# Block-sparse attention and an MLP on one core: the same operations in another order, with VectorE and GpSimd set differently against each other

## The chip, the cores and the metric

The kernel runs on one core of a Trainium2 chip. A core has five engines that work side by side, each through its own list of instructions in order: TensorE (PE in the profile; PEld is its loading of weights), VectorE (DVE), ScalarE (ACT), GpSimd (POOL) and SyncE (SP), which here only issues transfers. They wait for each other through semaphores. The metric is the device time of one execution in microseconds (us).

## The reference

Attention over q, k, v of shape (4, 8, 768, 64), then an MLP on its output. The keys are cut into 12 blocks of 64. For each query the mean key of every block gives a gate score; blocks later than the query's own are shut out; the three best blocks, and the query's own, are seen, causally:

```python
k_rep = k.reshape(B, H, n_blocks, block, D).mean(axis=3)
gate_scores = np.einsum('bhsd,bhnd->bhsn', q, k_rep)
gate_scores = np.where(causal, gate_scores, -1000000000.0)
top_idx = np.argsort(gate_scores, axis=-1)[..., -top_k:]
...
scores = np.where(mask, scores, -1000000000.0)   # mask: chosen or own block, and causal
attn = softmax(scores);  out = attn @ v
...
h = x @ w_in                                     # x: 3072 x 512, w_in: 512 x 2048
g = 0.5 * h * (1.0 + np.tanh(c * (h + 0.044715 * h * h * h)))
return (g @ w_out).astype(np.float32)            # w_out: 2048 x 512
```

## The kernel before

The work is tiled by pairs of heads: 4 batches of 4 pairs, pair p = 0 to 15. For each pair a preparation (`pre`) turns q and k so that the head dimension lies on the partitions, makes the block means, the gate scores, and from them the mask. After the four pairs of a batch its 768 tokens go through the MLP, while the next batch's pairs are prepared and attended.

The preparation of a pair, step by step, with the engine and the line in the file of before:

- the loads of k, q and v (`load`, L387 and L393, issued on SP). The first batch's are turned by PE (L541), with copies out of PSUM on DVE or ACT (`copy`, L356 on ACT, L358 on GpSimd, L360 on DVE). Later batches' q and k are turned by DVE (L557).
- block sums of the keys (L576, L614, DVE) and their place in a two-head matrix `ksb` (L582, L588, L631, DVE).
- the gate scores: eight small matmuls (L680, PE).
- the selection, on DVE: a transpose (L696, called gx below), adding the causal gate `cgate` (L703), the eight largest of each row (L712), a comparison with the third of them (L713), and the mask value `madd` with the own block let in by `ownm1` (L717). L703, L713 and L717 are two-input steps: both operands lie in SBUF.
- the mask, transposed by PE (L749; later batches by a transfer) and copied below the queries as 12 further rows, so that the score matmul adds it. The matching rows of the keys hold a constant matrix E, which says to which block a key belongs; SP copies it there (`fill`, L513).

The attention of a pair: score matmuls (L856 for batch 0, L1039 later), exp on ACT (L875, L1052), a causal cut of the diagonal blocks on GpSimd (`affine_select`, L901 and L1066, tile `ats`), the product with v (L924, L1078), the division by the sum (L942 and L943, L961 and L962, DVE), and a transpose of the output into the MLP's input `xT` (L981, PE).

The MLP: first product (L1115), gelu on ACT (L1127), second product. Batch 0 does this plainly (L1315). The others use seven products instead of eight for a 2 x 2 split (L1365, with sums of weights L1284 and of activations L1302 on DVE, and joins of the results L1414); batch 3 does part of its first product so too (L1163 to L1228). The weights `w_in` and `w_out` are each loaded in two halves from GpSimd's queue (`load_w`, L451 and L453). The load of `w_in` is started by a tiny copy on GpSimd that reads the last v of batch 0. On SP, a small transfer that reads the end of `w_in` (`hold`, L1560) keeps the loads of pair 4 and later back until `w_in` is there.

GpSimd also makes the constants: `emit_p(i)` zeroes the parts of buffer set i that nothing else writes (four memsets over L502 to L507), `gates` makes `cgate` and `ownm1` (L473 to L484), `e16` makes E (a memset L491 and two `affine_select` of L494).

Finally `warm` offers 72 matmuls on zeros (L1517); those that the order names keep TensorE busy in the beginning and fill some gaps.

What sets the order of everything is three tables written out in the file. Each step is an operation with a number. `ORDER` lists the numbers; `BUFFER` holds, in that order, which buffer a step takes where there are several; `ENGINE` names the steps that run on ACT or GpSimd in place of their first choice. Nothing is reordered afterwards: each engine, and each engine's queue of transfers, works in the order in which `Plan.run` emits.

```python
for n in ORDER:
    op = self.ops[n]
    for kind, key in op.takes:
        if key not in self.buf:
            self.buf[key] = self.kinds[kind][0][next(picks)]
    op.emit(engine.get(n, next(iter(op.engines))))
```

Of the kernel before, what the change touches and what calls it, by code (L numbers as in the profile page):

```python
# [182 lines left out]
    "POOL": [  # L183
        338, 586, 587, 646, 647, 707, 708, 972, 973, 1035, 1036, 1097, 1098,
        1159, 1160, 1425, 1426, 1488, 1489, 1550, 1551, 1612, 1613]}


class Op:
# [1431 lines left out]
```

## Time and profile before

| | before |
|---|---|
| median of 3 runs | 253.98 us (253.59 to 254.15) |
| the profiled execution | 254.11 us |
| its span, first to last instruction | 252.4 us |
| granted TensorE clock | 1.00 |
| busy: PE / DVE / ACT / POOL | 244.2 / 188.6 / 178.5 / 86.8 us |

The span is what the profile's rows cover; 1.7 us of the execution lie around it. A row of a timeline gives start, duration, engine, line, operation, the tiles out<-in, the shape, a count where several are drawn together, and in brackets how long the engine was idle before it and what ended that. A list of waits gives who waited for whom, total, times and the longest. A row of windows gives the busy time of each engine in a stretch. A row of a group gives the shortest, median and longest duration in ns.

### The profile page before, as it was taken

To read this page: it belongs to the slowest core of one execution; us is meant where nothing else is said; L and a number is where in the kernel's file an instruction comes from. 1 tells how busy PE (TensorE), PEld (TensorE's weight loads), DVE (VectorE), ACT (ScalarE), POOL (GpSimd) and SP (SyncE) were. 2 spreads that over 40 slices of the span, in tenths; PEclk is the share of its full clock that TensorE was granted. 3 is DMA by queue.
4 is the path that set the end of the run, shared out by engine and by line. 5 is a ranking of instruction groups with operands and counts; after the bars stand their busy time and mean duration, and the time that the engine had idled before them with its cause. 6 is when DMAs were issued, how large, how long until landed. Compare 5 with 4: busy or idle time off the path is not lost.

```text
span 252.4 us, 6423 instructions
## 1 busy us (share of the span) xinstructions
PE 244.2 (97%) x2483; PEld 170.4 (68%) x2483; DVE 188.6 (75%) x533; ACT 178.5 (71%) x225; POOL 86.8 (34%) x169
## 2 busy tenths in 40 slices
PE   7898999999999999999999999999999999999993
PEld 5665786555546666555778887656778887666883
DVE  2799863031869999999898977999775785687954
ACT  2577877546799999767899897757998927667300
POOL 8766860002135587240066644420244500000000
PEclk9999999999999999999999999999999999999999
DMA  8999599999999895999998996351601250020024
GB/s 153 219 207 184 88 211 180 214 151 160 141 153 130 155 198 93 146 176 181 167 204 145 223 154 114 88 118 42 166 4 24 41 180 20 3 84 0 4 92 158
DMA packets 130927, 32.62 MB, mean 129 GB/s; under 512 B 124528, under 2 KB 126928, under 8 KB 130896
## 3 DMA queue, kind: packets, MB, share of 16 engines
q1 hardware_dynamic: 126160, 27.62, 64.7%
q0 software_dynamic: 3136, 4.19, 10.0%
q10 hardware_dynamic: 1600, 0.39, 0.8%
q8 instruction: 19, 0.31, 0.6%
q14 instruction: 12, 0.10, 0.1%
HBM read 27.26 MB, written 6.29 MB: 133 GB/s over the span
## 4 chain that ended last, share of the span: by engine, by line
PE 91%; DVE 4%; DMA 2%; issue 1%; ACTq 1%; ACT 0%; DVEq 0%
PE wide L1115 27%; PE bank L1365 22%; PE wide L1039 11%; PE bank L1315 8%; PE bank L1078 6%; PE wide L1204 5%; PE wide L856 3%; PE bank L680 2%; PE bank L924 2%; DMA G<-in_q_dram 2%; PE bank L541 1%; PE bank L749 1%; PE bank L981 1%; DVE sel L712 1%; DVE sel L713 1%
## 5 line engine op out<-in xcount | busy, mean ns | idle before, releaser
L1115 PE MATMUL wide<-xT,w_in 128*128 128x384 f16 x416 | 74.1, 326 | 0.0
L1052 ACT ACTIVATE ats<-wide 128x896 f16<-128x896 f32 x72 | 62.0, 913 | 3.6 <-PE wide L1039 1.3
L1127 ACT ACTIVATE G<-wide 128x768 f16<-128x768 f32 x52 | 42.0, 809 | 27.0 <-PE wide L1115 25.3
L1115 PEld LDWEIGHTS <-w_in 128*128 128x128 f16 x416 | 39.9, 98 | 26.8 <-issue 1.3
L1066 POOL TENSOR_SCALAR_AFFINE_SELECT ats<-ats 128x256 f16<-128x256 f16 x72 | 31.3, 450 | 58.1 <-ACT ats L1052 57.8
L1039 PE MATMUL wide<-qT,kT 76*128 76x512 f16 (+3 forms) x192 | 38.6, 305 | 0.0
L557 DVE STREAM_TRANSPOSE s<-sd 128x768 f32<-128x768 f32 x24 | 23.2, 970 | 13.7 <-DMA sd<-in_k_dram 11.5
L1365 PE MATMUL bank<-w_out,G 128*128 128x256 f16 x216 | 31.9, 272 | 0.0
L1365 PEld LDWEIGHTS <-G 128*128 128x128 f16 x288 | 27.2, 98 | 5.2
L1315 PE MATMUL bank<-w_out,G 128*128 128x512 f16 x96 | 28.1, 379 | 0.0
L1414 DVE TENSOR_TENSOR osb<-bank,osb 128x512 f32<-128x512 f32 (+1 forms) x38 | 22.2, 594 | 7.0 <-PE bank L1365 6.5
L1039 PEld LDWEIGHTS <-kT 76*128 76x128 f16 x192 | 17.3, 97 | 10.6 <-issue 0.5
L875 ACT ACTIVATE ats<-wide 128x1024 f16<-128x1024 f32 (+3 forms) x24 | 21.0, 916 | 4.7 <-PE wide L856 4.6
L1078 PEld LDWEIGHTS <-ats 128*128 128x128 f16 x504 | 21.8, 97 | 3.6 <-POOL ats L1066 0.2
L358 POOL CAST kT<-s 64x768 f16<-64x768 f32 x23 | 19.5, 846 | 14.0 <-DVE s L557 13.2
L1078 PE MATMUL bank<-v,ats 128*128 128x65 f16 x504 | 24.1, 194 | 0.0
L1365 PEld LDWEIGHTS <-XS 128*128 128x128 f16 x216 | 20.0, 97 | 4.8
L1365 PE MATMUL bank<-TS,XS 128*128 128x256 f16 x144 | 22.8, 272 | 0.0
L358 POOL CAST v<-vsd 128x768 f16<-128x768 f32 x13 | 10.7, 828 | 30.9 <-DMA vsd<-in_v_dram 22.2
L356 ACT CAST qT<-s 64x768 f16<-64x768 f32 x21 | 17.4, 827 | 0.3
L962 DVE TENSOR_TENSOR xn<-bank,zr 128x384 f16<-128x384 f32 x24 | 13.4, 558 | 0.8
L712 DVE MAX8 sel<-sel 128x8 f32<-128x12 f32 x160 | 13.3, 157 | 0.6
(118 smaller groups left out, 350.3 us busy)
## 6 DMA issues: line engine op xcount, KB each, us to landing
out_dram<-osb SPq DMA_DIRECT2D x23, 256.0 KB
vsd<-in_v_dram SPq DMA_DIRECT2D x26, 192.0 KB
sd<-in_k_dram SPq DMA_DIRECT2D x48, 96.0 KB
sd<-in_q_dram SPq DMA_DIRECT2D x48, 96.0 KB
w_in<-in_moe_w_in_dram POOLq DMA_DIRECT2D x2, 1024.0 KB, 11.3
w_out<-in_moe_w_out_dram POOLq DMA_DIRECT2D x2, 1024.0 KB, 18.5
G<-in_q_dram SPq DMA_DIRECT2D x4, 192.0 KB
G<-in_k_dram SPq DMA_DIRECT2D x4, 192.0 KB
```

The lines of the kernel that those rows point to most:

```text
L358: nc.gpsimd.tensor_copy(out=out, in_=in_)
L557: nc.vector.transpose(out=T[key + "T32", p], in_=T[key, p].rearrange("p t j -> p (t j)"))
L875: nc.scalar.activation(out=T["at", u][:, :, 0:n], in_=plan.buf[("st",) + u].rearrange("p (h w) -> p h w", h=2)[:, :, 0:n], func=AF.Exp, bi ...
L1039: nc.tensor.matmul(st[:, x:e], kT16[i][h][0:76, s0:s0 + 128], qT16[i][h][0:76, s0 + (x - cb):s0 + (e - cb)], start=True, stop=True)
L1052: nc.scalar.activation(out=T["at", u][:, 0:n], in_=plan.buf[("st",) + u][:, 0:n], func=AF.Exp, bias=0.0, scale=SCALE)
L1066: nc.gpsimd.affine_select(out=dg, in_=dg, compare_op=ALU.is_ge, fill=0.0, base=0, pattern=[[0, 2], [1, 128]], channel_multiplier=-1)
L1078: nc.tensor.matmul(pvv[:, qc, 0:65], at[:, cb + (qc - jc) * 128: cb + (qc - jc + 1) * 128], v16[i][:, jc, h, :], start=(gi == 0 and jc == ...
L1115: nc.tensor.matmul(hps[:, 512 * e:512 * e + HALF], w_in16[:, ci, (2 * j + e) * 128: (2 * j + e + 1) * 128], T["xT", b][:, ci, HALF * h:HAL ...
L1127: nc.scalar.activation(out=G[:, :, h, j, :], in_=plan.buf["hps", b, j, h].rearrange("p (e w) -> p e w", e=2)[:, :, 0:HALF], func=AF.Gelu_a ...
L1315: nc.tensor.matmul(plan.buf["ops", b, ti], G[:, f % 2, 2 * ti // NC, f // 2, ti % (NC // 2) * 128:ti % (NC // 2) * 128 + 128], w_out16[:, ...
L1365: nc.tensor.matmul(dst[:, HD * h:HD * h + HD], FACT[m][0][:, j, t * 128:(t + 1) * 128], FACT[m][1][:, j, :], start=(clear and j == 0), sto ...
L1414: nc.vector.tensor_tensor(out=dst(), in0=src(), in1=other(), op=ALU.add)
```

## The change

Only the three tables change; the functions and so the operations are the same, and the file is one line shorter, so that line numbers after the tables are smaller by one. The core of the diff, the beginning of `ORDER` and all of `ENGINE`:

```diff
 ORDER = [
-    5, 2, 1890, 6, 1891, 1892, 1893, 9, 15, 0, 1894, 1895, 1896, 1897, 12,
-    1898, 1899, 1900, 22, 1901, 1902, 1903, 23, 1904, 1905, 1906, 71, 72,
-    62, 73, 195, 64, 63, 82, 75, 76, 66, 1907, 3, 77, 1908, 74, 1, 18, 1909,
...
+    1890, 3, 9, 1891, 1892, 1893, 1894, 1, 6, 15, 1895, 2, 1896, 1897, 1898,
+    195, 1899, 1900, 1901, 1902, 1903, 1904, 1905, 1906, 12, 1907, 71, 62,
+    64, 73, 72, 75, 0, 82, 76, 66, 77, 63, 1908, 1909, 74, 22, 23, 1910, 67,
+    1911, 98, 18, 68, 1912, 84, 85, 19, 100, 78, 31, 99, 194, 83, 79, 101,
...
     "ACT": [
-        63, 67, 74, 99, 101, 114, 119, 121, 345, 346, 349, 449, 467, 486,
-        504, 523, 541, 594, 595, 628, 654, 657, 715, 716, 719, 749, 893,
-        980, 981, 1043, 1044, 1105, 1106, 1167, 1168, 1202, 1433, 1434,
-        1496, 1497, 1558, 1559, 1668, 1674, 1677, 1704, 1707, 1727, 1733,
-        1736, 1786, 1822],
+        63, 67, 72, 74, 90, 94, 99, 101, 119, 121, 134, 331, 346, 449, 467,
+        486, 504, 523, 541, 594, 628, 654, 655, 657, 715, 716, 749, 929,
+        980, 981, 1043, 1044, 1105, 1106, 1167, 1202, 1346, 1433, 1434,
+        1496, 1668, 1677, 1698, 1704, 1727, 1733, 1736, 1786, 1822],
     "POOL": [
-        338, 586, 587, 646, 647, 707, 708, 972, 973, 1035, 1036, 1097, 1098,
-        1159, 1160, 1425, 1426, 1488, 1489, 1550, 1551, 1612, 1613]}
+        337, 586, 587, 646, 647, 707, 708, 972, 973, 1035, 1036, 1097, 1098,
+        1159, 1160, 1426, 1488, 1489, 1550, 1551, 1612, 1613]}
```

What this does to each engine's list, by the numbers:

- GpSimd's constants. Before: `emit_p(3)` (5), `emit_p(0)` (2), `gates` (0), `emit_p(1)` (3), `e16` (1), `emit_p(2)` (4), then cuts of `ats` and casts. After: `emit_p(1)` (3), `e16` (1), `emit_p(0)` (2), `gates` (0), one cut of `ats` (197), `emit_p(3)` (5), `emit_p(2)` (4), and the rest. The load of `w_out` (163) is issued behind three more cuts than before.
- SP's loads after the first five. Before: q2, k2, v0, half of k3, half of q3, half of k3, v1, half of q3, v2, v3. After: half of k2, q2, half of k2, v0, v1, q3, half of k3, half of v2, half of k3, half of v2, v3. Later loads change places as well (k6's first half ahead of q5, for instance).
- PE: the gate of pair 2 (122) stands behind one more product with v (208), one product with v (315) ahead of the first L1115; steps of the first batch change places throughout. 35 of the matmuls on zeros are used instead of 37; the two left out stood between real work.
- From ACT to DVE: 114 (a copy of k), 345, 595, 1168, 1497, 1558, 1559 (q as 16-bit, pairs 4 to 14), 349, 719 (mask copies of pairs 4 and 7), 893 (a result of the second product), 1674, 1707 (intermediate results of batch 3). From DVE to ACT: 72 (q of pair 0), 90, 94, 134 (k of pairs 1 and 3), 331 (`xT`), 655 (q as 16-bit, pair 6), 929, 1346 (results of the second product), 1698. From DVE to GpSimd: 337; from GpSimd to DVE: 338, 1425 (k as 16-bit).
- The end: the same steps in the same chain.

295 rows, old and new, of tables (BUFFER, ORDER) are left out of this document.

## The prediction

> **What bounds the kernel now.** I read the busy times first, then the windows, then the waits of TensorE, and last the timelines at the places the waits name. The page's first part, for the whole span:
>
> ```profile
> PE 244.2 (97%) x2483; PEld 170.4 (68%) x2483; DVE 188.6 (75%) x533; ACT 178.5 (71%) x225; POOL 86.8 (34%) x169
> ```
>
> PE is missing 8.2 us of 252.4. The windows (time, then width and PE busy, PEld, DVE, ACT, POOL, clock, DMA share, GB/s) show where:
>
> ```profile
> 5.00:10.00 5.00, 3.50 (x35) 2.75 (x33) 3.20 (x13) 1.44 (x3) 4.62 (x11) 1.00 1.37 219
> 15.00:20.00 5.00, 4.36 (x67) 2.96 (x65) 4.75 (x20) 4.61 (x6) 2.68 (x5) 1.00 0.97 207
> 20.00:25.00 5.00, 4.20 (x81) 3.07 (x76) 4.72 (x20) 3.28 (x4) 3.58 (x6) 1.00 1.05 180
> 75.00:150.00 75.00, 74.96 (x794) 51.42 (x793) 70.55 (x192) 66.88 (x86) 35.83 (x65) 1.00 1.05 165
> 240.00:252.40 12.40, 8.61 (x79) 7.47 (x77) 5.72 (x11) 0.00 (x0) 0.00 (x0) 1.00 0.35 127
> ```
>
> PE has holes in the front and in the tail; between them it is full, at full clock. So time can be won only in the front or by giving PE less to do; time can be lost wherever another engine falls behind. DVE is the one with little room: 70.55 of 75 us. The longest waits of PE (total, times, longest):
>
> ```profile
> PE bank L749 <- DVE madd L717: 1.8, 3, 0.8
> PE bank L1517 <- DVE bmask L285: 1.1, 1, 1.1
> PE bank L541 <- DMA G<-in_q_dram: 0.8, 1, 0.8
> ```
>
> The mask transposes (L749) wait for the selection chain on DVE (L696, L703, L712, L713, L717). In DVE's rows for that chain in the first pair, and then for three calls of L713 in 11 to 24 us (durations in ns):
>
> ```profile
> L703 DVE TENSOR_TENSOR sel<-sel,cgate x1: 714/714/714, 7.9 to 7.9; 128x48 f32<-128x48 f32 x1
> L713 DVE TENSOR_TENSOR sel<-sel,sel x1: 509/509/509, 9.1 to 9.1; 128x48 f32<-128x48 f32 x1
> L717 DVE SCALAR_TENSOR_TENSOR madd<-sel,ownm x1: 207/207/207, 9.7 to 9.7; 128x48 f16<-128x48 f32 x1
> ```
>
> ```profile
> L713 DVE TENSOR_TENSOR sel<-sel,sel x3: 234/285/750, 12.1 to 21.8; 128x120 f32<-128x120 f32 x2, 128x72 f32<-128x72 f32 x1
> ```
>
> A larger L713 (128x72) takes 0.23 us and 128x48 takes 0.51; the same 128x120 takes 0.285 or 0.75. GpSimd's rows of the same times:
>
> ```profile
> 6.88 0.74 POOL L491 MEMSET G<- 128x768 f16 x1
> 7.69 1.87 POOL L494 TENSOR_SCALAR_AFFINE_SELECT G<-G 64x768 f16<-64x768 f16 x2
> 9.62 0.16 POOL L502 MEMSET v<- 128x12 f16 x1
> 9.66 0.65 POOL L503 MEMSET madd<- 128x640 f16 x1
> ```
>
> The slow L703 starts at 7.9 and ends with the first of the two L494 (about 8.6); the slow L713 (9.11 to 9.62) ends with the second (9.56). L717 runs at 9.7 under a memset and is not held. So a DVE step with both inputs in SBUF stands still while GpSimd reads SBUF, and not while it only writes.
>
> **A rule beside this.** The Trainium skill, "SBUF — State Buffer", section "Who interferes with whom", says just this of two-input steps, and adds that whichever engine issues first keeps the port while the other blocks entirely. By that addition a held GpSimd would also hand its delay on; no row here shows a long held GpSimd instruction, and the sum below does without it.
>
> **The change, part by part.** All three tables are replaced; the instructions are the same but for two warm fillers.
>
> *GpSimd's constants.* Now: zeroing of buffers 3 and 0, gates, buffer 1, E, buffer 2. After: buffer 1, E, buffer 0, gates, then the first ats select, buffers 3 and 2. E (0.74 + 1.87) moves ahead of the first selection, whose start is given by PE. In the first chain L703 loses 714 − 234 = 0.48 and L713 509 − 234 = 0.28, 0.76 together (234 ns is a larger tile's time, so this is a floor). Gates comes last of the four and its own short selects may hold L703 a little: I take 0.7. The place of buffers 3 and 2 (memsets) behind the first ats select delays a cast of the mask by about 2.8 us at 13.4 us; its readers, the scores of pair 1, stand from 18 us on: nothing lost.
>
> *Front order and loads.* The rows that date the front now (two selections starting, a mask, the first v's landing):
>
> ```profile
> 14.06 0.35 DVE L696 STREAM_TRANSPOSE sel<-bank 128x160 f32<-128x160 f32 x1
> ...
> 20.26 0.34 DVE L696 STREAM_TRANSPOSE sel<-bank 128x160 f32<-128x160 f32 x1
> ```
>
> ```profile
> 9.99 0.29 PE L749 MATMUL bank<-ident,madd 128*128 128x128 f16 x2 [0.74 <-DVE madd L717]
> ...
> 31.25 0.45 PE L749 MATMUL bank<-ident,madd 128*128 128x128 f16 x5 [0.24 <-DVE madd L717]
> ```
>
> ```profile
> 16.83 0.83 POOL L358 CAST v<-G 128x768 f16<-128x768 f32 x1 [2.00 <-DMA G<-in_v_dram]
> ```
>
> On SP v1, q3 and v2's first half now go ahead of k3 or its second half. The loads take about 0.925 us per 192 KB half (estimate: from the first v, landed at 16.83, to the last, at 26.08 in the row below, are ten halves), so k3 lands at about 23.3, four halves later than now (19.6). Following the selections by hand with these rows' durations, mine is: first mask 9.2 to 9.3 (now 9.99), selection of pair 1 at 13.3 (now 14.06), of pair 2 at 19.0 (now 20.26; its gate stands behind one pv more), k3 23.3, gate 3 about 26.3, mask 3 about 29.0 (now 31.25), first MLP matmul (L1115) about 36.0 (now 38.24). A lead of 2.2 us, between 1 and 2.6. It's spent on weights:
>
> ```profile
> 26.08 0.19 POOL L451 COPY after_in<-vsd 1x16 f32<-1x16 f32 x1 [1.06 <-DMA vsd<-in_v_dram]
> 26.63 1.66 POOL L453 DMA_DIRECT2D w_in<-in_moe_w_in_dram  x2 [0.35 <-issue]
> ...
> 30.70 1.78 POOL L453 DMA_DIRECT2D w_out<-in_moe_w_out_dram  x2
> ```
>
> ```profile
> DMA to landing us min/median/max: 9.1/11.3/13.5
> ```
>
> ```profile
> DMA to landing us min/median/max: 16.1/18.5/21.0
> ```
>
> The first of these lines is w_in's, the second w_out's. w_in's second half is issued at 27.54 and lands at 41.0, w_out's first half at 30.70 + 16.1 = 46.8. The w_in issue waits for the last v load, which is last on SP in both orders, so it doesn't move. w_out's issue moves behind three more ats selects on POOL, to about 35; its data follow w_in's on the same queue, so it lands when it did as long as it's issued before w_in has landed at 41. PE now:
>
> ```profile
> 38.24 0.81 PE L1115 MATMUL wide<-xT,w_in 128*128 128x384 f16 x4
> ...
> 42.88 5.04 PE L1115 MATMUL wide<-xT,w_in 128*128 128x384 f16 x30
> 47.75 0.38 PE L1315 MATMUL bank<-w_out,G 128*128 128x512 f16 x1
> ```
>
> The pitch of L1115 is (47.75 − 42.88)/30 = 0.162. L1315, the first reader of w_out, comes 9.51 us after the first L1115, after the change 9.26 (one pv of 0.25 goes ahead of it). Started at 36.0, PE would want w_in's second half at 40.4, wait to 41.1, want w_out at 46.0, wait to 46.8. The work done by then is the same as at 47.75 now: of 2.2 us of lead **0.95** stays. Any lead of over 1 us gives the same.
>
> *Fillers.* 37 zero matmuls become 35; the two missing stood between real work, at about 0.11 each (the pitch of matmuls of the same 128x256, in the chain's last stretch): **−0.2**, from PE's full time.
>
> ```profile
> 232.31 16.20 PE bank L1365 x148
> ```
>
> *Copies changed over.* Twelve go from ACT to DVE (six of them q16, 0.56 each in the row below), nine the other way, one more comes to DVE from GpSimd; by the durations the same operations have in the trace DVE gets 2.5 us more. The place where this can reach PE is the last gate of batch 2:
>
> ```profile
> L360 DVE CAST qT<-s x3: 552/556/556, 77.7 to 188.6; 64x768 f16<-64x768 f32 x3
> ```
>
> ```profile
> 63.40:115.20 51.80, 51.76 (x492) 30.59 (x491) 47.19 (x143) 45.27 (x60) 24.80 (x42) 1.00 1.03 149
> ```
>
> ```profile
> 115.06 0.14 DVE L631 TENSOR_TENSOR ksb<-bmask,ks 128x32 f32<-128x32 f32 x1
> ```
>
> ```profile
> 114.95 0.79 PE L680 MATMUL bank<-s,ksb 128*32 128x160 f32 x16
> ```
>
> These are the gates of pairs 10 and 11, eight matmuls each, 0.31 apiece and overlapping: the second begins about 115.3, its ksb is ready at 115.2, so 0.1 us is left. After the change PE reaches this gate 0.5 us earlier counted from pair 4's, and DVE has 0.2 more to do (one q16 and two mask copies more, one q16 and one transpose for the weights less, one w_sums step more), while about 0.3 us of DVE's waiting for PE goes. 0.5 + 0.2 − 0.1 − 0.3 gives 0.3; with port holds as now, which grow where DVE has more two-input steps in GpSimd's company, I take **+0.5**. Bounds: 0, if DVE's 4.6 us of idle in that window give way, and 0.3 + 2.3 = 2.6, if a wait for a gate like the one now ahead of pair 5 is met once more:
>
> ```profile
> 71.48 0.35 DVE L696 STREAM_TRANSPOSE sel<-bank 128x160 f32<-128x160 f32 x1 [2.26 <-PE bank L680]
> ```
>
> *The tail* has the same chain: nothing.
>
> Sum: 254.11 − 0.95 − 0.2 + 0.5 = 253.46 for the profiled execution, which was 0.13 over the median of 253.98: **253.3**.
>
> **The rivals.** (a) The cap doesn't hold: with less on the DMA queues w_out lands a us or so earlier, or the later POOL issue matters less than I think. Then the whole lead of 2.2 counts: 252.1. Against it: nothing in the change moves w_in's issue. (b) The front wins nothing: k3's landing 3.7 us later holds gate 3 by more than I walked, and L1115 starts at 38.2 as now; 254.11 − 0.2 + 0.3 − 0.13 gives 254.1. For it: in the row of waits, loads already hold PE by 0.8. (c) The other side: DVE becomes the bound. It has 4.45 us idle in 75 to 150 us and takes on a part of the 2.5 us there. If the gate of pair 11 is missed by the upper bound, 2.6, what PE loses there isn't found again, as PE has no later hole: 254.11 − 0.95 − 0.2 + 2.6 − 0.13 = 255.4. It decides from a miss of 1.7 us (0.95 + 0.2 won, 0.5 of measurement); beyond 2.6 lies 256. (d) w_out's issue slips behind 41 us, because the ats selects ahead of it on POOL wait for exps that wait for PE: then each us of slip is a us of PE, and 5 us of slip lose all; with 36.85 as the present time of the last of these three selects it takes a front 4 us slower than now.
>
> **How the numbers follow.** The forecast, its terms within 0.5 us, gets 0.42; (a) 0.13; (b) 0.17; (c) 0.23; (d) 0.05. Range 252.2 to 255.8: it leaves out (d), the worst of (c) and a full uncapped lead. The likeliest case's own range is 252.8 to 253.9. A measurement of this kernel can tell about 0.2%, 0.5 us, from no change: faster means under 253.47, slower over 254.49. Faster: most of the forecast's case and (a), 0.46; same: the rest of it and most of (b), 0.21; slower: (c), (d) and a part of (b), 0.33.
>
> **What would show it.** Right: L703 and L713 of the first pair at about 0.23; L1115's first start near 36 and waits of PE for w_in and w_out, some 0.7 and 0.8, that the list now lacks; the first L1315 at 46.8; 35 L1517; in 75 to 150 us a new wait of PE for ksb of under a us. Wrong: first L1115 after 37.3; L1315 before 46.5; waits of PE for DVE that sum to over 1.7 us after 38 us.

## The result, and the profile after

The changed kernel is slower: 256.25 us (median of 6, 255.39 to 257.21) against 253.83 (median of 6), ratio 1.0095, 95% interval 1.0068 to 1.0123. The forecast was 253.3, range 252.2 to 255.8, and faster. The profiled execution of the changed kernel took 257.21 us, the slowest of the six, with a span of 255.5; what follows is its trace, 0.96 us over the median: shares of a loss that are read from it hold for this execution. Lines of the changed file are smaller by one.

Its busy times, and the slices of TensorE's granted clock:

```profile
PE 246.6 (97%) x2481; PEld 170.5 (67%) x2481; DVE 191.9 (75%) x537; ACT 175.0 (69%) x222; POOL 88.5 (35%) x168
...
PEclk9999999999999999999999999999979999999998
```

DVE is busy 3.3 us longer and ACT 3.5 less, near the forecast's 2.5 and a part of it holding. One slice of the clock, near 188 us, is new, and the last one is lower. The waits of PE:

```profile
PE bank L1077 <- POOL ats L1065: 1.6, 2, 1.1
PE bank L1516 <- DVE bmask L284: 1.1, 1, 1.1
PE bank L540 <- DMA G<-in_q_dram: 0.9, 1, 0.9
PE wide L1038 <- DVE qT L359: 0.4, 1, 0.4
PE bank L1364 <- DVE XS L1301: 0.3, 1, 0.3
PE bank L748 <- DVE madd L716: 0.3, 1, 0.3
PE bank L1314 <- DMA w_out<-in_moe_w_out_dram: 0.2, 1, 0.2
PE wide L1203 <- DVE s L359: 0.2, 1, 0.2
```

The mask wait (L748, 1.8 before) is down to 0.3. In its place stand waits that the list of before lacks, and the largest is for the causal selects of GpSimd (L1065). First the front, where the forecast looked. The first pair's selection, durations in ns, and PE around the start of the MLP:

```profile
L702 DVE TENSOR_TENSOR sel<-sel,cgate x1: 208/208/208, 8.0 to 8.0; 128x48 f32<-128x48 f32 x1
L712 DVE TENSOR_TENSOR sel<-sel,sel x1: 207/207/207, 8.7 to 8.7; 128x48 f32<-128x48 f32 x1
```

```profile
36.31 2.44 PE L1114 MATMUL wide<-xT,w_in 128*128 128x384 f16 x14
...
40.70 5.04 PE L1114 MATMUL wide<-xT,w_in 128*128 128x384 f16 x30
45.95 0.38 PE L1314 MATMUL bank<-w_out,G 128*128 128x512 f16 x1 [0.21 <-DMA w_out<-in_moe_w_out_dram]
```

The two steps that took 0.71 and 0.51 take 0.21 each. The first L1114 starts at 36.31 (38.24 before, and a product of 0.25 now lies ahead of it), the first reader of w_out at 45.95 (47.75): a lead of 1.8 us. PE keeps it: the first matmul of the second product of batch 1 starts at 119.75, against 121.90 before, 2.15 earlier. Then it goes. The first matmul of the second product of batch 2 starts at 176.47 against 177.31, 0.84 earlier; its first matmul of product 7 at 189.36 against 186.87, 2.5 later; the last join at 251.64 against 248.54, 3.1 later. So 1.3 us are lost between 120 and 176, 3.3 between 176 and 189, and 0.6 behind that; of this last part only one wait of 0.2 (L1203) stands on the list, and the rest was not followed up.

The 3.3 us, in rows of GpSimd, VectorE and PE:

```profile
180.74 4.07 POOL L1065 TENSOR_SCALAR_AFFINE_SELECT ats<-ats 128x256 f16<-128x256 f16 x3 [10.41 <-ACT ats L1051]
```

```profile
180.62 1.01 DVE L1301 TENSOR_TENSOR XS<-G,XS 128x768 f16<-128x768 f16 x2
181.56 1.48 DVE L1301 TENSOR_TENSOR G<-G 128x768 f16<-128x768 f16 x3
182.96 0.67 DVE L1413 TENSOR_TENSOR osb<-bank,osb 128x512 f32<-128x512 f32 x1
183.56 0.54 DVE L1301 TENSOR_TENSOR G<-G 128x768 f16<-128x768 f16 x1
184.13 0.85 DVE L359 COPY qT<-mT 12x640 f16<-12x640 f16 x2
```

```profile
183.36 0.39 PE L1077 MATMUL bank<-v,ats 128*128 128x65 f16 x7 [1.09 <-POOL ats L1065]
...
184.43 0.39 PE L1077 MATMUL bank<-v,ats 128*128 128x65 f16 x7 [0.46 <-POOL ats L1065]
```

Three selects take 4.07 us. As a group (shortest, median, longest in ns, of the changed kernel; then the same place before):

```profile
L1065 POOL TENSOR_SCALAR_AFFINE_SELECT ats<-ats x3: 478/1104/2563, 180.7 to 184.3; 128x256 f16<-128x256 f16 x3
```

```profile
L1066 POOL TENSOR_SCALAR_AFFINE_SELECT ats<-ats x5: 406/408/779, 180.7 to 185.0; 128x256 f16<-128x256 f16 x5
```

A select alone takes 0.41. The first starts at 180.74, when VectorE has just begun a string of five two-input steps (180.62 to 183.04). VectorE's steps are not slowed at all, 0.54 each; the select waits for the whole string, 2.56 us, and ends 0.27 after it, under L1413, which reads PSUM. The second select (1.10) meets the sum at 183.56 and again ends 0.27 after that has ended. This is the hold of the forecast in the other direction: GpSimd is the one that stands. And PE is left idle for 1.55 us, and behind that its clock is halved. In windows of 1 us (width, PE, PEld, DVE, ACT, POOL, clock):

```profile
184.00:185.00 1.00, 0.57 (x9) 0.43 (x10) 0.93 (x3) 0.00 (x0) 0.81 (x2) 1.00 0.00 0
185.00:186.00 1.00, 1.00 (x9) 0.65 (x7) 0.00 (x0) 0.70 (x1) 0.00 (x0) 0.77 0.00 0
186.00:187.00 1.00, 1.00 (x7) 0.70 (x5) 0.00 (x0) 0.75 (x2) 0.72 (x2) 0.50 0.00 0
187.00:188.00 1.00, 1.00 (x10) 0.66 (x8) 0.00 (x0) 0.38 (x1) 0.05 (x1) 0.50 0.07 16
188.00:189.00 1.00, 1.00 (x11) 0.60 (x9) 0.00 (x0) 0.92 (x1) 0.00 (x0) 0.52 0.00 0
189.00:190.00 1.00, 1.00 (x15) 0.87 (x14) 0.01 (x1) 0.60 (x1) 0.96 (x2) 1.00 0.00 0
```

0.23 + 0.50 + 0.50 + 0.48 gives 1.7 us. With the 1.55 that is 3.3. The half clock comes in some executions only. Lasting 3.41 us, it takes 0.007 off an execution's mean clock: two of the six have so low a mean (0.990 in the profiled one, 257.21 us, and 0.993 in the one of 256.99). The other four (255.39, 255.78, 255.99, 256.52) have 1.00 or 0.997, as executions of before have too, and their median, 255.9, is still 2.1 over before. So the half clock makes the profiled execution longer, and isn't what makes the kernel slower.

The Trainium skill, "TensorE: Matmul & The Clock Gate", part 1, says that the clock is halved after an idle window of some 3.4 us, windows running freely. The trace agrees with the length of the window: its records have the half clock from 185.54 to 188.95, 3.41 us, and the changes of the clock in this trace, at 4.63, 185.54, 188.95 and 253.81, lie whole multiples of 3.413 apart. It does not agree that the window must be idle throughout: the one before the change, 182.13 to 185.54, holds 1.55 us of idle, and the measurement decides.

The losses between 120 and 176 stand at PE's waits of 0.34 + 0.08 at 122 (sums, L1301) and 0.40 at 134.4 (a mask copy, L359). That is 0.8 of the 1.3; an experiment below finds the rest in the same places. VectorE and GpSimd ahead of the first, then at the second:

```profile
113.37 0.86 DVE L1301 TENSOR_TENSOR XS<-XS,G 128x768 f16<-128x768 f16 x1
114.16 1.30 DVE L1283 TENSOR_TENSOR w_out<-w_out 128x1024 f16<-128x1024 f16 x1
115.39 1.17 DVE L1301 TENSOR_TENSOR XS<-G,XS 128x768 f16<-128x768 f16 x1
...
133.74 1.02 DVE L359 COPY qT<-mT 12x640 f16<-12x640 f16 x1
```

```profile
113.00 1.92 POOL L357 CAST v<-vsd 128x768 f16<-128x768 f32 x2 [4.75 <-DMA vsd<-in_v_dram]
114.99 1.16 POOL L357 CAST kT<-s 64x768 f16<-64x768 f32 x1
...
133.76 0.83 POOL L357 CAST v<-vsd 128x768 f16<-128x768 f32 x1
```

Here the casts hold VectorE: sums of 0.55 take 0.86 and 1.17 (and a cast of 0.82 takes 1.16, so each holds the other). The mask copy, which has one input only, takes 1.02 where 0.32 is its time, and ends 0.17 after the cast.

### The profile page after: what moved, and what is told of

It reads as the page before. It is cut to its first block, busy times and chain, and to the rows that moved or that the text cites. A ratio compares the mean times of both kernels' runs of the same rounds, so it can differ in the third digit from the quotient of the medians.

```text
span 255.5 us, 6443 instructions
## 1 busy us (share of the span) xinstructions
PE 246.6 (97%) x2481; PEld 170.5 (67%) x2481; DVE 191.9 (75%) x537; ACT 175.0 (69%) x222; POOL 88.5 (35%) x168
## 4 chain that ended last, share of the span: by engine, by line
PE 78%; DMA 9%; DVE 5%; ACT 3%; POOL 2%; issue 2%; ACTq 1%; SPq 0%; DVEq 0%; POOLq 0%
PE wide L1114 21%; PE bank L1364 17%; PE wide L1038 9%; PE bank L1314 8%; PE bank L1077 6%; PE wide L1203 5%; DMA w_out<-in_moe_w_out_dram 4%; PE wide L855 3%; PE bank L679 2%; DMA vsd<-in_v_dram 2%; PE bank L923 2%; DMA G<-in_q_dram 2%; DMA mT<-madd 2%; POOL ats L1065 1%; ACT G L1126 1%
## 5 line engine op out<-in xcount | busy, mean ns | idle before, releaser
L1114 PE MATMUL wide<-xT,w_in 128*128 128x384 f16 x416 | 74.2, 326 | 0.0
L1114 PEld LDWEIGHTS <-w_in 128*128 128x128 f16 x416 | 40.0, 98 | 26.8 <-issue 1.2
L1065 POOL TENSOR_SCALAR_AFFINE_SELECT ats<-ats 128x256 f16<-128x256 f16 x72 | 32.9, 474 | 53.4 <-ACT ats L1051 53.2
L1038 PE MATMUL wide<-qT,kT 76*128 76x512 f16 (+3 forms) x192 | 39.5, 311 | 0.4 <-DVE qT L359 0.4
L1364 PE MATMUL bank<-w_out,G 128*128 128x256 f16 x216 | 32.7, 272 | 0.0
L1314 PE MATMUL bank<-w_out,G 128*128 128x512 f16 x96 | 29.2, 379 | 0.2 <-DMA w_out<-in_moe_w_out_dram 0.2
L1077 PE MATMUL bank<-v,ats 128*128 128x65 f16 x504 | 25.0, 195 | 1.6 <-POOL ats L1065 1.6
L1077 PEld LDWEIGHTS <-ats 128*128 128x128 f16 x504 | 22.6, 98 | 5.6 <-POOL ats L1065 2.3
L1413 DVE TENSOR_TENSOR osb<-bank,osb 128x512 f32<-128x512 f32 (+1 forms) x38 | 22.2, 591 | 3.3 <-PE bank L1364 2.7
L1364 PE MATMUL bank<-TS,XS 128*128 128x256 f16 x144 | 23.8, 273 | 0.4 <-DVE XS L1301 0.3
L355 ACT CAST qT<-s 64x768 f16<-64x768 f32 x16 | 13.2, 828 | 0.3
```

Of the source, the lines that this page charges most:

```text
L1038: nc.tensor.matmul(st[:, x:e], kT16[i][h][0:76, s0:s0 + 128], qT16[i][h][0:76, s0 + (x - cb):s0 + (e - cb)], start=True, stop=True)
L1065: nc.gpsimd.affine_select(out=dg, in_=dg, compare_op=ALU.is_ge, fill=0.0, base=0, pattern=[[0, 2], [1, 128]], channel_multiplier=-1)
L1077: nc.tensor.matmul(pvv[:, qc, 0:65], at[:, cb + (qc - jc) * 128: cb + (qc - jc + 1) * 128], v16[i][:, jc, h, :], start=(gi == 0 and jc == ...
L1114: nc.tensor.matmul(hps[:, 512 * e:512 * e + HALF], w_in16[:, ci, (2 * j + e) * 128: (2 * j + e + 1) * 128], T["xT", b][:, ci, HALF * h:HAL ...
L1314: nc.tensor.matmul(plan.buf["ops", b, ti], G[:, f % 2, 2 * ti // NC, f // 2, ti % (NC // 2) * 128:ti % (NC // 2) * 128 + 128], w_out16[:, ...
L1364: nc.tensor.matmul(dst[:, HD * h:HD * h + HD], FACT[m][0][:, j, t * 128:(t + 1) * 128], FACT[m][1][:, j, :], start=(clear and j == 0), sto ...
```

## The experiments

Theory 1: the front's lead is real, and the order of the rest loses it, at the places where VectorE's and GpSimd's instructions hold each other. Theory 2: the lead itself disturbs, because transfers come at fixed times. A rival to the hold at 181 us is that the selects are late for another reason, and one to the order is the engine moves.

**Front alone.** `ORDER` up to the first L1315 with its engines and buffers from the changed kernel, the rest from before:

```diff
-ORDER (before)
+changed ORDER up to operation 433, then what is left of the order of before
```

> The changed order up to and with the first L1315, then everything that is left in the order, on the engines and in the buffers of before. Theory 1 (the front's lead is real, and what is lost later is lost by the new order of the rest): the lead of 1.8 us after 46 us stays to the end, no new waits behind it; 253.83 - 1.8 = 252.0 us. Theory 2 (the lead itself is what disturbs: a PE that is 1.8 us ahead meets transfers and exps that come at fixed times): the waits seen at 122, 135 and 183 us come back in this kernel too, and it ends at 254 or above.

253.33 us, ratio 0.9983 (0.9974 to 0.9992). Faster, but by 0.5 where 1.8 was expected; no wait of 122, 135 or 183 came back. The list of PE's waits names the rest:

```profile
PE wide L1115 <- ACT G L1127: 0.9, 1, 0.9
```

That stands at 46.6, where the two orders are joined: two first products follow each other in one PSUM tile. So the seam was to blame, and was mended:

```diff
-rest: wide tile 0, 1 as before; gelu 407 behind the seam
+rest: wide tile 1, 0; gelu 407 ahead of operation 393
```

> As e1_front, where PE waited 0.90 us at 46.6 for a gelu: at the seam two first products follow each other in the same PSUM tile. Here the rest takes the other of the two tiles, and one gelu stands ahead of the seam. If that wait is all that separates e1_front from the full lead, 253.3 - 0.9 = 252.4 us, with the lead of 1.4 to 1.8 us kept to the end. If a lead is lost in any case to w_out or to the fixed times of transfers: 253.0 or more.

252.58 us, ratio 0.9959 (0.9944 to 0.9974), as expected. The lead is worth 1.2 us to the end by the medians, 1.5 by the profiled executions, where PE waits 0.50 for w_out at 46.2; behind 47 it has no wait over 0.1 us. Theory 2 falls.

**Rest alone.** Before up to operation 464, then the changed order.

> The order of before up to the last matmul of the first L1315 row's second token tile (operation 464, about 53 us of PE work), then what is left in the changed order. Theory 1: no lead in front, and the same losses behind it, 4.2 us by the medians (256.25 - 253.83 + 1.8): 258.0 us. Theory 2: without the lead no loss: about 254.

257.56 us, ratio 1.0150 (1.0130 to 1.0171). GpSimd's row at the same place:

```profile
183.30 4.26 POOL L1065 TENSOR_SCALAR_AFFINE_SELECT ats<-ats 128x256 f16<-128x256 f16 x3 [10.82 <-ACT ats L1051]
```

The stall is there without any lead (1.7 us in two waits), together with 0.8 for a copy at 68, near the place where the orders are joined. In its profiled execution the clock stayed at 1.00, with as much idle time. Counted in steps of 3.413 us from its first change of the clock (5.38), the two waits fall into two windows, 1.28 us of idle in one and 0.46 in the next, and not into one. That this is why is not shown: in before, a window of its own count with 1.78 us of idle (246.98 to 250.39) left the clock at 1.00 as well.

**The string broken.** The four sums of product 7 behind one join and two copies on VectorE:

```diff
-    1252, ..., 1276, ..., 1277, ..., 1301, ..., 1253, ..., 1320, ..., 1229, ..., 1624, ..., 1563
+    1252, ..., 1276, ..., 1320, ..., 1624, ..., 1563, 1277, 1301, 1253, 1229
```

> The changed kernel with the four activation sums of product 7, batch 2 (L1301, G<-G, at 181.6 to 184.1 us) moved behind one join and two copies on VectorE, nothing else. Theory 1 (the string of two-input steps on VectorE holds GpSimd's selects, the first of them 2.56 us instead of 0.41): that select ends about 182.1, PE's waits for ats of 1.6 us go, and with them the stretch of lower clock behind them; 256.25 - 2.5 = 253.7, to 253.2 if the clock dip counts in full. Rival (the selects are late because exp or their own place in GpSimd's order is late): no more than 0.3 us.

253.86 us, ratio 0.9993 (0.9981 to 1.0005): 2.4 us less than the changed kernel, by four instructions in another place. In this first form product 7 was emitted ahead of the sums and read its factor without them; the second form mends that:

> As e3_m7late, where product 7 read its factor before the four sums were written (its output was not the reference's); here they stand behind the join and the two copies, and ahead of product 7. Nothing waits for the sums before 189 us, so the same time: 253.8 us, PE's waits for ats gone, first select under 1.3 us.

253.90 us, ratio 1.0012 (0.9993 to 1.0032). Its rows:

```profile
180.08 2.08 POOL L1065 TENSOR_SCALAR_AFFINE_SELECT ats<-ats 128x256 f16<-128x256 f16 x3 [10.82 <-ACT ats L1051]
```

```profile
180.15 1.01 DVE L1301 TENSOR_TENSOR XS<-G,XS 128x768 f16<-128x768 f16 x2
181.09 0.68 DVE L1413 TENSOR_TENSOR osb<-bank,osb 128x512 f32<-128x512 f32 x1
181.78 0.90 DVE L359 COPY qT<-mT 12x640 f16<-12x640 f16 x2
182.69 2.17 DVE L1301 TENSOR_TENSOR G<-G 128x768 f16<-128x768 f16 x4
```

Two two-input steps hold the first select (1.35 us at most in the group, 0.05 over what was expected), the join that reads PSUM lets all three through by 182.16, and the string comes when PE does not wait for a select. PE's wait for ats is gone. The rival falls: the first select starts 4.27 us behind the first matmul of the second product in both kernels (180.74 and 176.47, 180.08 and 175.81), so exp is no earlier here.

Two more things stand in these rows. The select starts 0.07 us ahead of the two steps and is held by them all the same, so the starts of rows do not tell which engine had the port. And where the moved string is met by two more selects, the first is let in:

```profile
183.78 1.35 POOL L1065 TENSOR_SCALAR_AFFINE_SELECT ats<-ats 128x256 f16<-128x256 f16 x2 [1.61 <-ACT ats L1051]
```

The two take 0.67 and 0.72. The first ends at 184.45, 0.27 after the third sum, while the fourth, which starts at 184.10, takes 0.76 instead of 0.55. So a select can get in between two sums; what decided it here and not at 180.74 in the changed kernel is open.

**Two casts moved as well.**

```diff
-    ... 1094 on GpSimd, at 113.0 ...   1156, ..., 1160
+    815, 1094, ..., 791 (1094 on ScalarE)   1160, 1156
```

> As e6_m7valid, with two of GpSimd's casts moved: the cast of v of pair 10 (113.0 us) to ScalarE, where it stood idle from 113.5 to 114.7, and the cast of v of pair 11 (133.8) behind two other instructions on GpSimd. If GpSimd's casts hold VectorE there, and that makes PE's waits of 0.42 for sums at 122 and of 0.40 for a mask copy at 134.4: both shrink to under 0.2, the mask copy takes 0.32 instead of 1.02; 253.0 us. If VectorE is simply short of time in that stretch: no change, 253.8.

252.59 us, ratio 0.9958 (0.9944 to 0.9972). The waits at 122 and 134.4 are gone, and the mask copy is short:

```profile
115.50 0.55 DVE L1301 TENSOR_TENSOR XS<-G,XS 128x768 f16<-128x768 f16 x1
...
133.27 0.32 DVE L359 COPY qT<-mT 12x640 f16<-12x640 f16 x1
```

It gained 1.3 us on the previous kernel, where its two waits were 0.26 + 0.08 and 0.41. The other 0.5 stands in the same places. The first row and the last of the same 154 matmuls, in the previous kernel and then in this one:

```profile
119.16 0.82 PE L1364 MATMUL bank<-w_out,G 128*128 128x256 f16 x6
134.55 0.38 PE L1364 MATMUL bank<-TS,XS 128*128 128x256 f16 x2
```

```profile
120.03 0.82 PE L1364 MATMUL bank<-w_out,G 128*128 128x256 f16 x6
134.16 0.38 PE L1364 MATMUL bank<-TS,XS 128*128 128x256 f16 x2
```

That is 15.39 against 14.13, 1.26 less. The brackets count a wait from the drawn end of the matmul before it; back to back the next one would have started ahead of that end, about 0.16 earlier (a 128x256 matmul is drawn with 0.27, and they follow each other every 0.11). Three stops cost 0.5 more than their brackets say.

From 119.75 on the changed kernel and this one run the same 1257 matmuls in the same order, so their starts can be laid side by side. The changed kernel falls back 0.7 us at 122, 0.6 at 134.8, 1.9 at 183.4 to 184.4 and 1.7 under the half clock, 4.9 in all, and nowhere else by more than 0.1. (The last two make 3.6; against before, whose matmuls stand in another order there, it was 3.3.)

Six moved steps, and ScalarE for one of them, turn the changed kernel from 2.4 us slower than before into 1.2 faster. By the medians this kernel and e5_front_flip are the two fastest of all that were run.

**The engine moves undone, behind the front.**

```diff
-ENGINE behind operation 433: changed
+ENGINE behind operation 433: as before
```

> The changed order and buffers, with the eighteen engine moves behind the first L1315 undone (copies back to ScalarE and GpSimd as before, four back to VectorE). If the loss comes from VectorE having more copies (the prediction's rival with the gates as its place): 254.0 or less. If it comes from the order, with VectorE's string of sums at 180.6 us untouched: the first select there still takes over 2 us, and the time is 255.5 or more.

257.99 us, ratio 1.0142 (1.0104 to 1.0180). By the median 1.7 us more than the changed kernel, with intervals that overlap, and not less; the longest select is 2.39 us with its PE wait of 0.9. So the copies given to VectorE are not the loss. In this order they may even save time: without them PE has waits for ScalarE (exp 0.8, q as 16-bit 0.7) that the changed kernel lacks.

**What makes the lead.** Three parts of the front, one at a time. GpSimd's constants as before, on the front with the unmended seam:

```diff
-    3, ..., 1, ..., 2, ..., 0, ..., 197, ..., 5, 4
+    5, ..., 2, ..., 0, ..., 3, 1, 4, ..., 197
```

> As e1_front, with GpSimd's constants in the order of before (buffers 3, 0, gates, buffer 1, E, buffer 2). If the constants make the first part of the lead: L702 and L712 of the first pair take 0.71 and 0.51 again, the first mask is at 9.9 instead of 9.2, the first L1114 comes 0.7 later than in e1_front, and of that 0.3 is left behind the wait for w_out: 252.3. If only the order of the other steps and loads counts: no different from e1_front.

253.61 us, ratio 0.9995 (0.9982 to 1.0007), 0.28 more than e1_front with intervals that overlap. The steps were slow again (0.53 and 0.50), but the first L1115 started at 36.36, only 0.13 later than in e1_front (36.23): expected were 0.7. What the constants win at 9 us was made good by 36. The loads of batch 0, and the copies of q and k:

```diff
-loads on SP: k2a q2 k2b v0 v1 q3 k3a v2a k3b v2b v3
+loads on SP: q2 k2 v0 k3a q3a k3b v1 q3b v2 v3
```

> As e5_front_flip, with the loads of batch 0 on SP in the order of before (k3 four halves earlier, v1 and q3 later). If the new order of loads makes part of the lead: the first L1115 comes later than 36.3, towards 38.2, and the time is 253.2 or more. If the loads were never what PE waited for behind 10 us: the first L1115 stays within 0.3 us of 36.3 and the time at 252.6. I expect the second; the waits of PE in the front are for masks.

253.44 us, ratio 0.9995 (0.9982 to 1.0008), 0.9 more than e5_front_flip. My expectation was wrong: PE waited 0.5 for q of pair 3, and the first L1115 came at 37.08, 0.78 later.

```diff
-ENGINE of the front: 72, 90, 94, 134, 331 on ACT, 114 on DVE
+ENGINE of the front: 72, 90, 94, 134, 331 on DVE, 114 on ACT
```

> As e5_front_flip, with the six engine moves of the front undone (operations 72, 90, 94, 134 and 331 back on VectorE, 114 back on ScalarE), the order as it is. VectorE gets about 1.9 us of copies back before 37 us, where it is busy 4.4 to 4.9 of every 5 us between 10 and 30. If the moves carry the lead: the masks come 0.5 to 1.5 us later, the first L1115 at 37 to 38, the time 253.2 to 254. If the order alone carries it: first L1115 within 0.3 us of 36.3, 252.6.

267.53 us: a fault of the trial. One copy of `xT` stood on VectorE behind a transpose that waits for a load:

```profile
54.69 0.98 DVE L556 STREAM_TRANSPOSE s<-sd 128x768 f32<-128x768 f32 x1 [13.74 <-DMA sd<-in_k_dram]
55.59 0.32 DVE L359 COPY xT<-bank 128x384 f16<-128x384 f16 x1
```

> As e11_oldfrontengines, with the one copy of xT (331) left on ScalarE: on VectorE it stood in the order behind a transpose that waits for the load of pair 4 (54.7 us), and PE waited 11.8 us for it, which is a fault of that trial and tells nothing of the front. What is left undone are the five copies of q and k before 25 us. The first L1114 came at 37.37 in e11, 1.07 later than in e5; so here too, and the time is 252.6 + 1.07 less what the wait for w_out (0.5 in e5) takes up: 253.2 us. If the five copies don't matter: 252.6.

253.14 us, ratio 0.9972 (0.9961 to 0.9983): the first L1114 at 37.40, 1.1 later than in e5_front_flip. Loads (0.8) and copies (1.1) carry the 1.9 us between them, if they add, which no run shows; the constants next to nothing.

**Two fillers fewer.**

```diff
-    ..., 1924, ..., 1925, ...
+    (left out)
```

> As e5_front_flip without the two matmuls on zeros that stood between real work behind 200 us, as the changed kernel is without them. They are 0.11 us each of PE's own time: 252.58 - 0.22 = 252.36, if nothing had hidden them; no change, if PE waits there anyway.

252.75 us, ratio 0.9960 (0.9943 to 0.9977): no gain that shows. At 0.2 it is within what these runs can tell.

## Why the prediction was wrong, point by point

*Constants and the first selection:* the mechanism was right, to 0.05 us (0.21 each instead of "0.23"), the first mask came at 9.3. But it was not what carries the front: the terms were strung into one chain, and the trial without them shows that the chain has slack behind.

*The front's lead:* right in size. First L1115 "about 36.0", measured 36.31; no waits for masks but 0.3. The step "nothing lost" for the later memsets of buffers 3 and 2 held. Not foreseen is who made it, new loads and copies on ScalarE; of the loads I said only that k3 comes later.

*The cap by w_out:* its place was right, its size not. The forecast had 1.25 us eaten by two weight waits and 0.95 left; PE waited 0.21 for w_out and not for w_in, and 1.8 was left. The step that erred here is "The w_in issue waits for the last v load, which is last on SP in both orders, so it doesn't move": it moved from 26.63 to 26.14, w_in was there at 40.2 (41.0), w_out at 45.9. That w_out's later issue costs nothing (30.70 to 35.02) was right. This error made the forecast too slow, by 0.85.

*Fillers, −0.2:* neither shown nor refuted.

*Copies changed over:* here the forecast failed, and with it its sign. It priced all that the rest of the new order could do by one place, copies on VectorE that press on the gate of pair 11, for 0.5 us, with 2.6 as the bound. That gate (PE at 112.6) had no wait at all, and the moves undone did not make the kernel faster. What pressed instead was the order: three casts of GpSimd put at 113 to 116 beside two-input sums, a fourth at 133.8 beside a mask copy, and a string of sums put where the first selects of batch 3 come. This cost 0.42 + 0.40 + 1.55 in waits by the brackets, 3.2 by the starts of the matmuls, and in the profiled execution 1.7 more in clock. Waits of PE for VectorE behind 38 us, the forecast's sign of being wrong here, sum to 1.0 only, under its 1.7: the largest wait was for GpSimd.

*GpSimd held by VectorE* is the term that the forecast put at nothing: "the sum below does without it". The reason given was that no row shows "a long held GpSimd instruction". One did: in before, two selects beside three L1302 take 1.24 instead of 0.82, one of them 779 ns. The sentence beside the row, from the Trainium skill, "SBUF — State Buffer", section "Who interferes with whom", that whichever issues first keeps the port, was the one that spoke against this change, and it was set aside. The trace agrees with it in that VectorE's steps went on untouched at 181 us. That a select can have to outwait a whole string (2.56 us), not the one step that it met, no sentence of the forecast considered.

*The rivals:* (a) came true in part, 1.8 of 2.2 us counted. (c) had the sign right and VectorE as a part of it, and its place, its price and its reason wrong. The range ended at 255.8, the measured 256.25 lies 0.45 outside. The half clock does not excuse it: the four executions without it have a median of 255.9.

## What to carry to other kernels

Where an engine pair holds each other, count both directions: look for strings of two-input VectorE steps that cover the moment at which a short GpSimd instruction is due, and put the string behind steps that let it in (here a join that reads PSUM, and two copies). A hold of that kind cost nothing in before, where a select of 0.78 us kept no one waiting, and 1.9 us at a place where TensorE waited for the select, with 1.7 more in an execution in which the clock followed. When a reordered kernel is slower, join its first part to the rest of the old one and the other way round: two runs told here which part gained and which lost, once the seam itself was free of a wait.

## What the runs showed of the hardware that was not expected

A GpSimd select that met back-to-back two-input steps on VectorE had to wait for all of them in these four kernels: 2.56 us instead of 0.41 in a string of five, 2.75 with the changed rest alone, 2.39 with the engine moves undone, 1.35 with a string of two in e6_m7valid. It ended some 0.27 us after the string each time, and in e6_m7valid another select was let in between two sums. A VectorE copy with one input in SBUF (12x640, 16-bit) was held by a GpSimd cast, 1.02 instead of 0.32, and 0.32 again with the cast elsewhere. TensorE's clock fell to 0.50 for 3.41 us behind a window of 3.41 us with 1.55 us of idle; 1.74 us of idle over two such windows in another kernel, and 1.78 in one window of before, left it at 1.00.
